# Attention and MLP on one core: a second set of row buffers, casting loads by GpSimd, and two more batches transposed by DMA

## The chip, the cores and the metric

The kernel runs on one core of a Trainium2 chip. The metric is device time in microseconds (us) from start to end of one execution. Before the change: 357.96 us, the median of three runs (357.25 to 358.84). The names of the engines are those of the profile: PE is TensorE's matrix part and PEld its weight loads, DVE is VectorE, ACT is ScalarE, POOL is GpSimd, SP is SyncE, which only issues transfers here.

## What is computed

Selective attention is followed by a layer norm and a two-layer MLP with a residual. There are 8 batches (B), 8 heads (H), 576 positions (S), 64 per head (D), so a model width of 512 and a hidden width of 2048.

```python
# attention, per batch and head
cum = np.cumsum(np.maximum(s, 0.0), axis=-1)
scores = scale * q @ k.T + np.minimum(-(cum[:, None] - cum[None, :]), 0.0)
scores = np.where(causal, -1e9, scores)
x = softmax(scores) @ v                     # heads side by side: (8, 576, 512)
# the MLP, per row
xn = (x - mean) / np.sqrt(var + 1e-6) * g_ln
out = x + np.maximum(xn @ w_ch1, 0.0) @ w_ch2
```

All inputs and the output are float32; the kernel multiplies in bfloat16.

## The kernel before, in words

**Heads and groups.** The 64 heads are numbered n = 0 to 63, eight to a batch. Four heads make a group, `gam` = 0 to 15; group `gam` serves the heads from n = 4 `gam` on. Scores need K and Q with the 64 dimensions on the partitions. They lie in `kq`, three tiles, of which two alternate (`home`, L90): group `gam` uses `kq[gam % 2]`, apart from group 2, which has `kq[2]`. Four extra rows next to the 64 carry the bias of the cumulative sum (`cT`), so one matmul of 68 rows gives score plus bias.

**Where K and Q come from.** Groups 0 to 4 (`NPE = 5`) are transposed on PE, in a start that is written out step by step (`PLAN`, L950). From group 5 on the way is: token rows (128 positions, both of k and q, four heads: a tile t; five tiles to a group, the last of 64 positions) are loaded as float32 by SyncE's queue (`ld_rows`, L170, two transfers to a tile), cast to bfloat16 into `rows[t]` by GpSimd and given their bias columns from `cT` by GpSimd (`cast_rows`, L190), and transposed by a DMA transpose of SyncE's queue into `kq` (`tr_rows`, L205, one per tile). `NHW = 16` makes this the way of all groups 5 to 15. There is one set of five row tiles: `rows` (L95) lies in `kq[2]`, which is free after group 2. Their unused columns are zeroed once (`pre(14)`, L853). A function for casting during the load by GpSimd's own queue exists (`ld_cast_rows`, L181, with `bias_of_rows`, L199), but is not reached.

**The order.** All queues run in program order, which the code writes out by hand (`manual_schedule`). The main loop (L979) goes over n from 18 to 63. For each head: `pre(n)` (loads and, by a table in n - 4 `gam`, row tiles of a coming group); the scores and their exp on ACT, and the causal mask on GpSimd (`affine_select`, L366, L396); units of the MLP; `post(n)` (casts and transposes of a coming group); one more unit; PV and its normalisation of the head two before (`pv_next`, L889); and, in the second to fourth head of a batch, the layer norm of the batch before. The remaining units that are due for this head close it (L1011).

**Tables in n - 4 `gam`.** Loads: heads -6 (tiles 0, 1), -5 (2, 3), -4 (4). Casts, in `post`: -5 (0, 1), -4 (2, 3), -3 (4). Transposes, in `post`: -4 (0, 1), -3 (2, 3, then 4). V of the next batch is cast during its load by GpSimd's queue (`ld_cast_v`, L163), one tile per head over five heads.

**The MLP as filler.** A batch gives 32 units: 16 of the first matrix (`mlp1`, L533, four matmuls of 512 columns, L537, and a relu) and 16 of the second (`mlp2`, L551, four matmuls, L555; the fourth unit of a tile adds the residual on DVE, `yo`, L564, and stores it by SyncE's queue, L582). They are spread over the heads of the next batch so that PE never runs out; `end` and `nu` (L983, L984) say how many come per head and when the next batch's units are added.

**Layer norm.** `ln_xn` (L483) makes the normalised rows `xn` of one tile on DVE (L499). For the MLP they are transposed to `xT`: on PE through PSUM with a copy (`ln_tr`, L520; matmuls at L526) for batches up to 5, by SyncE's queue (`ln_tr_dma`, L516) for batches 6 and 7. The constant `NXD = 6` decides. Where PE transposes, all five `ln_xn` come in the second head of the batch (h = 1) and the transposes in the third and fourth; where the queue does, norm and transpose come together, three tiles in the second head and two in the third. Even batches have four tiles here, odd ones five: the last 64 positions of two batches share a tile.

Lines of the main loop that the change alters, before:

```python
            if b > 2 and h == 1:
                for t in range(NT):
                    ln_xn(b - 1, t)
            for t in {2: (0, 1), 3: (2, 3, 4)}.get(h, ()):
                ln_tr(b - 1, t, "act" if b == 2 else "dve")
                if t != 1 and t != 4:
                    run_units(1)
                    nu -= 1
```

Of the kernel before, what the change touches and what calls it, by code (L numbers as in the profile page):

```python
# [15 lines left out]
P = 128  # L16
# [3 lines left out]
def kernel(  # L20
# [11 lines left out]
    nc = tc.nc  # L32
    B, H, S, D = q.shape
# [6 lines left out]
    NT = NF + 1  # L40
# [3 lines left out]
    KA = D + 4  # L44
    OB, OC, OD = 512, 1024, 1536
    EW = 1664
    G = 4
    NG = BH // G
    NPE = 5
    NM = 10  # L50
    NHW = 16
    NXD = 6
    KT = 96
    QT = 6
    QP = S // QT
# [34 lines left out]
    def home(gam):  # L90
        return 2 if gam == 2 else gam % 2


    spare = kq[2].rearrange("p u h s -> p (u h s)")
    rows = [  # L95
        spare[:, i * 2 * G * P : (i + 1) * 2 * G * P].rearrange(
            "p (u h c) -> p u h c", u=2, h=G
        )
        for i in range(NT)
    ]  # L100

    er = const.tile([P, 4, EW], BF16, name="er")
    cT = const.tile([P, NT, 2, BH, 4], BF16, name="cT")
    xm = [const.tile([P, Dm], F32, name=f"xm{i}") for i in range(4)]
# [3 lines left out]
    zeros = const.tile([P, 512], BF16, name="zeros")  # L108

    rowb = const.tile([P, NT, 2 * H, KA], BF16, name="rowb")  # L110

    def copy_on(eng, out, in_):
        if eng == "act":
            nc.scalar.copy(out=out, in_=in_)
        elif eng == "dve":
            nc.vector.tensor_copy(out=out, in_=in_)  # L116
        else:
            nc.gpsimd.tensor_copy(out=out, in_=in_)


    loaded = {}
# [37 lines left out]
    def ld_cast_pair(g):  # L159
        ld_cast("k", g)  # L160
        ld_cast("q", g)
# [8 lines left out]
    def ld_rows(gam, t):  # L170
        pn = P if t < NF else TL
        b, h0 = gam // 2, (gam % 2) * G
        tmp = stage.tile([P, 2, G, D], F32, name="rowtmp", tag="st")
        for u, src in enumerate((k, q)):
            nc.sync.dma_start(  # L175
                out=tmp[0:pn, u],
                in_=src[b, h0 : h0 + G, t * P : t * P + pn, :].rearrange("h s d -> s h d"),
            )
        loaded["rows", gam, t] = tmp

    def ld_cast_rows(gam, t):  # L181
        pn = P if t < NF else TL
        b, h0 = gam // 2, (gam % 2) * G
        for u, src in enumerate((k, q)):
            nc.gpsimd.dma_start(
                out=rows[t][0:pn, u, :, 0:D],
                in_=src[b, h0 : h0 + G, t * P : t * P + pn, :].rearrange("h s d -> s h d"),
            )

    def cast_rows(gam, t):  # L190
        pn = P if t < NF else TL
        nc.gpsimd.tensor_copy(  # L192
            out=rows[t][0:pn, :, :, 0:D], in_=loaded.pop(("rows", gam, t))[0:pn]
        )
        nc.gpsimd.tensor_copy(
            out=rows[t][0:pn, :, :, D:KA], in_=cT[0:pn, t, :, gam * G : (gam + 1) * G, :]
        )

    def bias_of_rows(gam, t):  # L199
        pn = P if t < NF else TL  # L200
        nc.vector.tensor_copy(
            out=rows[t][0:pn, :, :, D:KA], in_=cT[0:pn, t, :, gam * G : (gam + 1) * G, :]
        )

    def tr_rows(gam, t):  # L205
        pn = P if t < NF else TL
        o = t * 2 * G * P
        nc.sync.dma_start_transpose(  # L208
            out=kq[home(gam)]
            .rearrange("p u h s -> p (u h s)")[:, o : o + 2 * G * pn]  # L210
            .rearrange("p (h s) -> p h s", s=pn),
            in_=rows[t][0:pn].rearrange("p u h c -> p (u h c)"),
        )

    w1_r = moe_w_ch1.rearrange("(kd p) dh -> p kd dh", p=P)
# [6 lines left out]
    def ld_w2(i):  # L222
        nc.gpsimd.dma_start(
            out=w2_bf[:, 4 * i : 4 * i + 4, :], in_=w2_r[:, 4 * i : 4 * i + 4, :]
        )
# [3 lines left out]
    def aug(gam, eng, h0=0):  # L229
        r = slice(gam * G + h0, gam * G + G)  # L230
        i = home(gam)
        eng.dma_start(out=kq[i][D : D + 1, 1, h0:G, 0:S], in_=c_hi[r, :])
        for j in range(3):
            eng.dma_start(out=kq[i][D + 1 + j : D + 2 + j, 0, h0:G, 0:S], in_=c3[r, j, :])
# [214 lines left out]
    def x_tiles(b):  # L449
        ts_ = [xb[b][:, t, :] for t in range(NF)]  # L450
        if b % 2 == 1:
            ts_.append(xm[b // 2])
        return ts_
# [20 lines left out]
    def ln_rstd(b):  # L474
        n = len(x_tiles(b))
        rs = rstd[:, b, 0:n]
        nc.vector.tensor_scalar_add(out=rs, in0=mvs[b][:, 0:n, 1], scalar1=1e-6)  # L477
        nc.gpsimd.tensor_tensor(out=rs, in0=rs, in1=mhalf[:, 0:n], op=ALU.pow)  # L478

    def ln_aggr(b, t):  # L480
        nc.vector.bn_aggr(out=mvs[b][:, t, :], in_=st[b][:, t, 0 : 2 if b == 0 else 3, :])

    def ln_xn(b, t):  # L483
        tiles = x_tiles(b)
        if t >= len(tiles):
            return
        if b == 0:
            nc.vector.tensor_scalar(
                out=mean0[:, t : t + 1],
                in0=sum0[:, t, 0:1],  # L490
                scalar1=sum0[:, t, 1:2],
                scalar2=1.0 / Dm,
                op0=ALU.add,
                op1=ALU.mult,
            )
        else:
            ln_aggr(b, t)
        xn = xnp.tile([P, Dm], BF16, name="xn", tag="xn")
        nc.vector.scalar_tensor_tensor(  # L499
            out=xn,  # L500
            in0=tiles[t],
            scalar=mvs[b][:, t, 0:1] if b > 0 else mean0[:, t : t + 1],
            in1=gb,
            op0=ALU.subtract,
            op1=ALU.mult,
        )
        xns[b, t] = xn
        if b > 0 and t == len(tiles) - 1:
            ln_rstd(b)
# [6 lines left out]
    def ln_tr_dma(b, t):  # L516
        if (b, t) in xns:
            nc.sync.dma_start_transpose(out=xT_dst(b, t), in_=xns.pop((b, t)))
# [77 lines left out]
    def run_units(n, dve_first=False):  # L596
        for i in range(n):
            if queue:
                first_unit[0] = dve_first and i == 0
                queue.pop(0)()  # L600
# [28 lines left out]
    for i in range(2):  # L629
# [9 lines left out]
        out=maskT,  # L639
        in_=maskT,  # L640
# [209 lines left out]


    def pre(n):
        if n == 14:  # L853
            for r in rows:
                nc.gpsimd.memset(r[:, :, :, KA:P], 0.0)
        if n in PAIR_LOADS:
            ld_cast_pair(PAIR_LOADS[n])
        if n in (11, 12):
            ld_w2(n - 9)
        if n in (8, 9):  # L860
            aug(n - 5, nc.sync)
        for gam in range(NPE, NG):
            m = n - 4 * gam
            ts_ = {-6: (0, 1), -5: (2, 3), -4: (4,)}.get(m, ())
            for t in ts_:
                if gam < NHW:
                    ld_rows(gam, t)
                else:
                    ld_cast_rows(gam, t)
                    bias_of_rows(gam, t)  # L870
            if gam >= NHW:
                for t in {-4: (0, 1), -3: (2, 3, 4)}.get(m, ()):
                    tr_rows(gam, t)
        for nb in range(2, B):
            t = n - H * nb + (5 if nb == 2 else 6)
            if 0 <= t < NT:
                ld_cast_v(nb, t)

    def post(n):
        for gam in range(NPE, NHW):  # L880
            m = n - 4 * gam
# [7 lines left out]
    def pv_next():  # L889
# [5 lines left out]
        if ph_ == 7:  # L895
# [6 lines left out]
            out=c_in[:, 0:P], in0=c_in[:, 0:P], scalar=0.0, in1=eight, op0=ALU.max, op1=ALU.mult  # L902
# [24 lines left out]
            out=c_in[:, P:S], in_=c_in[:, P:S], func=ACT.Relu, scale=1.0 / scale  # L927
# [51 lines left out]
    for n in range(2 * H + 2, BH):  # L979
        b, h = n // H, n % H  # L980
        pre(n)

        end = next(m for m in [8 * i + (3 if i <= NXD else 4) for i in range(2, B)] + [BH + 3] if m >= n)  # L983
        nu = -(-len(queue) // (end - n + 1)) - 2  # L984
        scores(b, h)
        run_units(1, True)
        if h % 2 == 0:
            scores_d(b, h // 2)
        post(n)
        run_units(1)  # L990
        pv_next()
        pend.append((b, h))
        if b <= NXD:
            if n == 2 * H + 2:
                for t in range(3, NT):
                    ln_xn(1, t)
            if b > 2 and h == 1:
                for t in range(NT):
                    ln_xn(b - 1, t)
            for t in {2: (0, 1), 3: (2, 3, 4)}.get(h, ()):  # L1000
                ln_tr(b - 1, t, "act" if b == 2 else "dve")
                if t != 1 and t != 4:
                    run_units(1)
                    nu -= 1
        elif h in (1, 2):
            for t in ((0, 1, 2), (3, 4))[h - 1]:
                ln_xn(b - 1, t)
                ln_tr_dma(b - 1, t)
                run_units(1)
                nu -= 1  # L1010
        run_units(nu)  # L1011
        if n == end:
            run_units(len(queue))
            queue += batch_units(b - 1)
# [41 lines left out]
```

## Time and profile before

| | |
|---|---|
| median of three runs | 357.96 us |
| the profiled execution | 358.78 us |
| its span in the profile | 357.1 us |
| granted clock of PE | 1.00 |
| busy: PE, DVE, ACT, POOL | 349.3, 196.2, 185.5, 162.2 us |
| PE transposes of `xn` (L526) | 108 matmuls |
| casts of rows on POOL (L192) | 55 |
| row loads on SyncE (L175) | 110 issues, median 0.51 us (k), 0.53 us (q) |
| row transposes on SyncE (L208) | 55 issues, median 1.29 us |
| `xn` transposes on SyncE (L518) | 9 issues, median 1.22 us |
| a head in the main loop | about 4.6 us |

How to read it: the span is what the profiler saw of one execution; what lies around it makes the rest of that execution's own time. A busy share says how much of the span an engine had an instruction in work, not that it held anything up. What held something up is read from the waits (engine and line that waited, and what ended the wait) and from the chain that is followed back from the last instruction. SPq and POOLq are the instructions by which a queue issues transfers: the time of an issue is not the time of the transfer.

### The profile page before, as it was taken

To read this page: it belongs to the slowest core of one execution; us is meant where nothing else is said; L and a number is where in the kernel's file an instruction comes from. 1 tells how busy PE (TensorE), PEld (TensorE's weight loads), DVE (VectorE), ACT (ScalarE), POOL (GpSimd) and SP (SyncE) were. 2 spreads that over 40 slices of the span, in tenths; PEclk is the share of its full clock that TensorE was granted. 3 is DMA by queue.
4 is the path that set the end of the run, shared out by engine and by line. 5 is a ranking of instruction groups with operands and counts; after the bars stand their busy time and mean duration, and the time that the engine had idled before them with its cause. 6 is when DMAs were issued, how large, how long until landed. Compare 5 with 4: busy or idle time off the path is not lost.

```text
span 357.1 us, 8417 instructions
## 1 busy us (share of the span) xinstructions
PE 349.3 (98%) x3154; PEld 198.9 (56%) x3154; DVE 196.2 (55%) x535; ACT 185.5 (52%) x359; POOL 162.2 (45%) x344
## 2 busy tenths in 40 slices
PE   8999999999899999999999999999999999999995
PEld 3899666555455555555565555555555544444444
DVE  7788888944376536844384539543764582113111
ACT  4899886577434763267336743475366403402500
POOL 9997669458436742582556452665341010000000
PEclk9999999999999999999999999999999999999999
DMA  9999999999979998699979974999740043011013
GB/s 151 170 180 171 199 190 166 191 192 168 184 147 204 153 212 149 106 226 172 171 129 213 207 145 84 222 180 174 158 119 2 0 80 113 0 61 60 0 32 89
DMA packets 169098, 49.73 MB, mean 139 GB/s; under 512 B 157744, under 2 KB 164448, under 8 KB 169056
## 3 DMA queue, kind: packets, MB, share of 16 engines
q1 hardware_dynamic: 116016, 36.53, 53.6%
q0 software_dynamic: 51600, 11.87, 37.1%
q10 hardware_dynamic: 1440, 0.79, 0.8%
q8 instruction: 25, 0.41, 0.5%
q14 instruction: 17, 0.14, 0.1%
HBM read 37.11 MB, written 9.44 MB: 130 GB/s over the span
## 4 chain that ended last, share of the span: by engine, by line
PE 84%; DVE 6%; DMA 3%; SPq 3%; POOL 2%; issue 1%; ACT 1%; DVEq 0%; POOLq 0%; ACTq 0%
PE py L555 31%; PE ph L537 29%; PE pot L424 6%; PE sc L346 3%; PE sb L346 3%; PE sa L346 3%; PE ph L817 2%; DVE xn L499 2%; DMA kq<-kq 2%; PE st L715 2%; SPq L175 1%; DMA rowtmp<-in_q_dram 1%; PE trx L526 1%; SPq L208 1%; PE pot L773 1%
## 5 line engine op out<-in xcount | busy, mean ns | idle before, releaser
L555 PE MATMUL py<-w_bf,hT 128*128 128x512 bf16 (+1 forms) x592 | 135.5, 373 | 0.4 <-DVE yo L564 0.4
L537 PE MATMUL ph<-xT,w_bf 128*128 128x512 bf16 x480 | 114.0, 379 | 0.0
L547 ACT ACTIVATE hT<-ph 128x512 bf16<-128x512 f32 x101 | 60.2, 597 | 74.3 <-PE ph L537 74.3
L555 PEld LDWEIGHTS <-hT 128*128 128x128 bf16 x592 | 53.7, 98 | 50.7 <-issue 0.9
L537 PEld LDWEIGHTS <-w_bf 128*128 128x128 bf16 x544 | 48.7, 97 | 50.5 <-issue 3.1
L366 POOL TENSOR_SCALAR_AFFINE_SELECT er<-er 128x256 bf16<-128x256 bf16 x108 | 43.7, 419 | 53.2 <-ACT er L357 52.3
L357 ACT ACTIVATE er<-sa 128x512 bf16<-128x512 f32 x56 | 33.3, 595 | 64.9 <-PE sa L346 50.3
L545 DVE TENSOR_SCALAR hT<-ph 128x512 bf16<-128x512 f32 x35 | 24.2, 692 | 57.3 <-PE ph L537 52.4
L192 POOL CAST kq<-rowtmp 128x512 bf16<-128x512 f32 (+1 forms) x55 | 33.5, 609 | 29.3 <-DMA rowtmp<-in_q_dram 27.4
L346 PEld LDWEIGHTS <-kq 68*128 68x128 bf16 x412 | 29.7, 97 | 23.5 <-DMA kq<-kq 2.0
L424 PEld LDWEIGHTS <-er 128*128 128x128 bf16 x840 | 32.8, 98 | 11.9
L436 DVE RECIPROCAL rinv<-pot 128x5 f32<-128x5 f32 x56 | 10.7, 192 | 50.0 <-PE pot L424 49.8
L564 DVE SCALAR_TENSOR_TENSOR yo<-py,rstd,xb 128x512 f32<-128x512 f32 x32 | 24.0, 749 | 24.2 <-PE py L555 19.5
L424 PE MATMUL pot<-v_bf,er 128*128 128x65 bf16 x840 | 34.7, 194 | 0.0
L165 POOL DMA_DIRECT2D v_bf<-in_v_dram x40 | 34.4, 867 | 0.3 <-DVE kq L116 0.3
L357 ACT ACTIVATE er<-sb 128x512 bf16<-128x512 f32 x56 | 33.5, 598 | 1.3 <-PE sb L346 1.3
L357 ACT ACTIVATE er<-sc 128x512 bf16<-128x512 f32 x56 | 34.1, 610 | 0.0
L478 POOL TENSOR_TENSOR rstd<-rstd,mhalf 128x4 f32<-128x4 f32 (+1 forms) x8 | 8.9, 1115 | 45.0 <-DVE rstd L477 45.0
L438 DVE TENSOR_TENSOR xb<-pot,rinv 128x256 f32<-128x256 f32 x56 | 23.8, 424 | 1.9
L346 PE MATMUL sb<-kq 68*128 68x64 bf16 (+1 forms) x156 | 21.4, 241 | 1.7 <-DMA kq<-kq 1.7
L462 DVE BATCH_NORM_STATS2 stats<-xb 128x6 f32<-128x128 f32 (+1 forms) x84 | 21.9, 320 | 0.3
L346 PE MATMUL sc<-kq 68*128 68x256 bf16 (+1 forms) x200 | 21.7, 226 | 0.1
(116 smaller groups left out, 354.2 us busy)
## 6 DMA issues: line engine op xcount, KB each, us to landing
out_dram<-yo SPq DMA_DIRECT2D x32, 256.0 KB
rowtmp<-in_k_dram SPq DMA_DIRECT2D x44, 128.0 KB
rowtmp<-in_q_dram SPq DMA_DIRECT2D x44, 128.0 KB
v_bf<-in_v_dram POOLq DMA_DIRECT2D x32, 128.0 KB, 6.1
w_bf<-in_moe_w_ch_dram POOLq DMA_DIRECT2D x8, 512.0 KB, 9.1
kq<-kq SPq DMA_TRANSPOSE x55
kp<-in_k_dram POOLq DMA_DIRECT2D x6, 144.0 KB, 8.7
qp<-in_q_dram POOLq DMA_DIRECT2D x6, 144.0 KB, 8.8
```

Source lines behind the costliest of these rows:

```text
L165: nc.gpsimd.dma_start(out=v_bf[b % 2][:pn, t, :, 0:D], in_=v[b, :, t * P : t * P + pn, :].rearrange("h s d -> s h d"),)
L192: nc.gpsimd.tensor_copy(out=rows[t][0:pn, :, :, 0:D], in_=loaded.pop(("rows", gam, t))[0:pn])
L346: nc.tensor.matmul(a[:, c + a0 - q0 : c + a1 - q0], lhsT=k_cols(b, h, kb), rhs=cols, start=True, stop=not (pe_mask and diag),)
L357: nc.scalar.activation(out=e[:, o : o + 512], in_=a, func=ACT.Exp, scale=scale)
L366: nc.gpsimd.affine_select(out=two, in_=two, compare_op=ALU.is_ge, fill=0.0, base=0, pattern=[[0, 2], [1, P]], channel_multiplier=-1,)
L424: nc.tensor.matmul(pot[:, t, :], lhsT=e[:, o : o + P], rhs=vv[:, kb, h, :], start=(kb == 0), stop=(kb == last),)
L438: nc.vector.tensor_tensor(out=xb[b][:, :, hs], in0=pot[:, 0:NF, 0:D], in1=rinv[:, 0:NF].unsqueeze(2).to_broadcast([P, NF, D]), op=ALU.mult,)
L537: nc.tensor.matmul(ph, lhsT=w1_bf[:, kd, fb * P : (fb + 1) * P], rhs=xT[:, kd, :], start=(kd == 0), stop=(kd == KD - 1),)
L545: nc.vector.tensor_scalar_max(out=hT[:, fb, :], in0=ph, scalar1=0.0)
L547: nc.scalar.activation(out=hT[:, fb, :], in_=ph, func=ACT.Relu)
L555: nc.tensor.matmul(py[t], lhsT=hT[:, fb, t * P : (t + 1) * P], rhs=w2_bf[:, fb, c0:c1], start=(fb == 0), stop=(fb == FB - 1),)
L564: nc.vector.scalar_tensor_tensor(out=yo, in0=py[t], scalar=rs, in1=x[:, c0:c1], op0=ALU.mult, op1=ALU.add)
```

## The change

It has three parts that share constants.

- **Two sets of row tiles.** `rows` becomes two sets of five tiles: one where it was, in `kq[2]`, one in `rowb`, the row buffer of the start, which is free by then. Group `gam` uses `rows[gam % 2]`. The unused columns of both are zeroed, in `pre(13)` and `pre(15)`.
- **Casting loads from group 7 on.** `NHW` goes from 16 to 7. Groups 5 and 6 keep SyncE's loads and GpSimd's casts. Groups 7 to 15 are loaded and cast by transfers on GpSimd's queue, their bias columns are copied by DVE, and their transposes are issued in `pre` instead of `post`. Group 6's loads come one head later in program order.
- **Normalised rows of batches 4 to 7 by SyncE's queue.** `NXD` goes from 6 to 4, so batches 4 and 5 join 6 and 7. The head after which a batch's units are added (`end`) moves one head later for batches 4 and 5. For the batches that stay on PE, the norms after the first two batches are split into three tiles in the second head and two in the third, with a unit between.

```diff
-    NHW = 16
-    NXD = 6
+    NHW = 7
+    NXD = 4
...
-    rows = [
-        spare[:, i * 2 * G * P : (i + 1) * 2 * G * P].rearrange(
-            "p (u h c) -> p u h c", u=2, h=G
-        )
-        for i in range(NT)
-    ]
+    rows = [
+        flat[:, 0 : NT * 2 * G * P].rearrange("p (t u h c) -> p t u h c", t=NT, u=2, h=G)
+        for flat in (spare, rowb.rearrange("p t h c -> p (t h c)"))
+    ]
...
# in ld_cast_rows, cast_rows, bias_of_rows, tr_rows:
-                out=rows[t][0:pn, u, :, 0:D],
+                out=rows[gam % 2][0:pn, t, u, :, 0:D],
...
     def pre(n):
-        if n == 14:
-            for r in rows:
-                nc.gpsimd.memset(r[:, :, :, KA:P], 0.0)
+        if n in (13, 15):
+            for t in range(NT):
+                nc.gpsimd.memset(rows[(n // 2 + 1) % 2][:, t, :, :, KA:P], 0.0)
...
-            ts_ = {-6: (0, 1), -5: (2, 3), -4: (4,)}.get(m, ())
+            ts_ = {-6: (0, 1), -5: (2, 3), -4: (4,)}.get(m - (gam < NHW and gam > NPE), ())
...
-            if b > 2 and h == 1:
-                for t in range(NT):
-                    ln_xn(b - 1, t)
+            for t in {1: (0, 1, 2), 2: (3, 4)}.get(h, ()) if b > 2 else ():
+                ln_xn(b - 1, t)
+                if t in (1, 2, 4):
+                    run_units(1)
+                    nu -= 1
             for t in {2: (0, 1), 3: (2, 3, 4)}.get(h, ()):
                 ln_tr(b - 1, t, "act" if b == 2 else "dve")
-                if t != 1 and t != 4:
+                if t not in (1, 4) and nu > 0:
                     run_units(1)
                     nu -= 1
```

The functions that the change now reaches are in the kernel before: `ld_cast_rows` (L181) and `bias_of_rows` (L199). The table for their transposes, in `pre`, is there as well (L871 to L873): heads -4 (tiles 0, 1) and -3 (2, 3, 4).

More of the change, by code (lines that the diff above doesn't have):

```diff
@@ L192, in cast_rows @@
         nc.gpsimd.tensor_copy(
-            out=rows[t][0:pn, :, :, 0:D], in_=loaded.pop(("rows", gam, t))[0:pn]
+            out=rows[gam % 2][0:pn, t, :, :, 0:D], in_=loaded.pop(("rows", gam, t))[0:pn]
         )
         nc.gpsimd.tensor_copy(
-            out=rows[t][0:pn, :, :, D:KA], in_=cT[0:pn, t, :, gam * G : (gam + 1) * G, :]
+            out=rows[gam % 2][0:pn, t, :, :, D:KA], in_=cT[0:pn, t, :, gam * G : (gam + 1) * G, :]
         )
@@ L201, in bias_of_rows @@
         nc.vector.tensor_copy(
-            out=rows[t][0:pn, :, :, D:KA], in_=cT[0:pn, t, :, gam * G : (gam + 1) * G, :]
+            out=rows[gam % 2][0:pn, t, :, :, D:KA], in_=cT[0:pn, t, :, gam * G : (gam + 1) * G, :]
         )
@@ L211, in tr_rows @@
             .rearrange("p (h s) -> p h s", s=pn),
-            in_=rows[t][0:pn].rearrange("p u h c -> p (u h c)"),
+            in_=rows[gam % 2][0:pn, t].rearrange("p u h c -> p (u h c)"),
         )
```

## The prediction, made before the result was known

> **What bounds the kernel now.** I read the page from its first part down. TensorE (PE) is busy almost all the time, and the chain that ended last is mostly PE.
>
> ```profile
> PE 349.3 (98%) x3154; PEld 198.9 (56%) x3154; DVE 196.2 (55%) x535; ACT 185.5 (52%) x359; POOL 162.2 (45%) x344
> ...
> PE 84%; DVE 6%; DMA 3%; SPq 3%; POOL 2%; issue 1%; ACT 1%; DVEq 0%; POOLq 0%; ACTq 0%
> ```
>
> So a microsecond taken from PE's instruction list, or from a wait of PE, is a microsecond of the span; work on the other engines is free while it stays hidden. Then PE's waits, of which the largest stands alone:
>
> ```profile
> PE sb L346 <- DMA kq<-kq: 1.7, 1, 1.7
> PE idle L607 <- DVE warm L620: 1.3, 1, 1.3
> PE py L555 <- DVE yo L564: 0.4, 2, 0.2
> ```
>
> The PE timeline places the first at head n=24, the first head of group 6: the second score matmul finds the last tile's transpose not landed.
>
> ```profile
> 91.00 0.38 PE L346 MATMUL sa<-kq 68*128 68x512 bf16 x1
> 93.08 0.39 PE L346 MATMUL sb<-kq 68*128 68x64 bf16 x3 [1.71 <-DMA kq<-kq]
> ```
>
> One `sa` to the next `sb` is 0.22 us elsewhere (140.04 minus 139.82), so the stall costs 93.08 - 91.00 - 0.22 = 1.86 us. The chain, cut to 60 to 96 us, tells what made the tile late: SyncE's queue (SPq), which runs group 5's transposes, then group 6's loads, then group 6's transposes without a pause.
>
> ```profile
> 69.94 1.22 SPq L208
> 71.16 0.05 issue
> 71.21 0.57 SPq L175
> ...
> 75.24 1.88 SPq L175
> 77.16 4.14 DMA rowtmp<-in_q_dram
> ...
> 86.97 6.07 DMA kq<-kq
> 93.04 0.05 issue
> 93.08 0.39 PE sb L346 x3
> ```
>
> Next the PE timeline around head 34 (batch 3 being normalised). A tile's four PE transposes take 142.95 - 142.72 = 0.23 us of PE (0.22 at 143.81), as matmuls overlap; the 219 ns of the group's row is the length of one. The `py` after the scores starts late, because VectorE (DVE) does five `xn` in a row (140.53 to 144.9) before the `yo` that frees PE's buffer.
>
> ```profile
> 142.72 0.39 PE L526 MATMUL trx<-ident,xn 128*128 128x128 bf16 x4
> 142.95 1.03 PE L555 MATMUL py<-w_bf,hT 128*128 128x512 bf16 x4
> ...
> 145.34 0.39 PE L346 MATMUL sc<-kq 68*128 68x256 bf16 x4
> 145.94 0.81 PE L555 MATMUL py<-w_bf,hT 128*128 128x512 bf16 x3 [0.21 <-DVE yo L564]
> ```
>
> The same happens at 221.6, with batch 5. 145.94 - 145.34 against a usual 0.22 to 0.23 (140.48 - 140.25) makes 0.37 lost each time.
>
> **The change part by part.**
>
> *Normalised rows of batches 4 and 5 leave PE* (6 and 7 had left already, so "4 to 7" adds two batches). Batch 4 has 4 tiles, batch 5 has 5: 9 x 4 = 36 matmuls of L526 go; 9 x 0.225 = **-2.0 us**, all on the path, since PE is full there (55.79 of 56 us between 168 and 224). 9 copies out of PSUM on DVE (414 ns) go too, hidden. SyncE gets 9 transposes at 1.22 us (median of L518). What hides them is distance: the first unit of batch 4 now comes after head 44, that of batch 5 after head 52. Batch 6 shows the same pattern already: its transposes are issued 255.2 to 262.8, the first `ph` that reads them starts at 265.25, without a wait. If that cover went, PE would wait once per batch.
>
> The Trainium skill bears here ("VectorE: DVE Perf Modes", The three transpose paths): it gives 390 ns for a 128x128 bf16 transpose on TensorE against 1309 ns on the DMA path, and advises TensorE where PSUM will do, which speaks against this edit. By its figure, an estimate, 36 x 0.39 = 14 us would leave PE and the forecast would be about 342; the timeline's 0.23 us for four decides. The price of the slower path is paid on SyncE's queue, where this trace has its own rows.
>
> *Norms split over two heads, with a unit after them.* In the built order the `yo` now stands behind three `xn` instead of four or five. 2 x 0.37 can go; the trace gives a loss of nothing to 0.2 as the other end if another DVE order brings a new wait. I take **-0.6**.
>
> *Two row buffers, filled by GpSimd's casting transfers from group 7 on.* Removed: 90 loads on SyncE (medians 0.51 and 0.53 us) and 9 x (4 x (0.610 + 0.208) + 0.604 + 0.203) = 37 us of GpSimd (POOL) casts and copies. Added to POOL: 90 transfers. The nearest rows are a half v tile, as many 256-byte pieces (0.69 at 57.76 and at 85.11), and L157's shortest, 0.63: 9 x (8 x 0.69 + 2 x 0.65) = 61 us. POOL's net is +24 us on 89.5 of the 173 us between 95 and 268, so 66% busy. POOL's queue holds the masks, and behind a mask waits PV of that head. A head takes 4.6 us and PV runs two heads after its scores; the densest head gets 4 x 0.69 + 0.89 + 1.06 of masks = 4.7 us, the next but one 2.4. The lag stays under one head: cost 0. Also added: 45 copies on DVE, about 0.19 us each (the 187 ns of its 128x24 copy): 8.5 us minus the 9 x 0.41 above, on an engine 60% busy; they wait for transposes of two groups earlier. Cost 0.
>
> Does a group still arrive in time? Tile 4's loads issue about when its pre(4*gam-4) comes; landing takes 6.0 us (median of L165; 4.1 to 15.9), then three transposes at 1.29 and 6.07 (the landing above): 1.4 + 6.0 + 3.9 + 6.1 = 17.4 at worst in a row, against 4 heads = 18.5. The first three overlap the loads in part, so I count 3 to 5 us of margin. Cost 0; the upper end is the rival below.
>
> *Group 6.* Its loads, casts and transposes remain, but SyncE issues transposes 0 and 1 before tile 4's loads (they wait for the casts only), and group 7's ten loads leave SyncE. By the rows: queue free at 71.2; out 0.5; eight loads and an out as now, to about 78.2; two transposes to 81; tile 4's loads to 82.4; transposes 2, 3 to 85.5; the load landed at 82.4 + 4.1 = 86.5, cast and copied 87.3; transpose 4 at 87.3 with less queued ahead of it than the 6.07 had, say 4.5: 91.8, against 91.22 where PE asks. Stall 0.6 instead of 1.86. Against it: ten memsets instead of five put 5 x 0.513 = 2.6 us more on POOL before group 5's casts, in a stretch where POOL is 84% busy (16.77 of 20). If all of it comes through, the stall becomes 4.4. Ends: -1.86 and +2.6. The first transposes were slow for another reason (L208's longest, 3.64, starts at 60.8, while v loads land), so I lean to the good end: **-0.9**.
>
> *Sum:* 357.1 - 2.0 - 0.6 - 0.9 = 353.6 us of span. The profiled execution took 358.78, 1.68 outside its span, and was 0.82 above the median of 357.96. So 355.3 against the profile, **354.5** against the median.
>
> **The rivals.**
>
> *The group 6 stall is gone altogether* and nothing else shows up: 357.96 - 2.0 - 0.74 - 1.86 = 353.4. It is the good end of the forecast.
>
> *Memsets late, stall grows.* POOL's 2.6 us go through group 5's casts and SyncE's queue to head 24: 357.96 - 2.6 + 2.6 = 358.0. For it: POOL runs without a gap from 52 to 64.6. Against it: the 3.64 above, which was no cast's fault. With half of it, 356.7. Chance 0.22, no change.
>
> *It does not take PE's work away in effect*: the freed 2.0 us turn into a wait of PE for `hT` or `yo`, since ACT and DVE set the pace of the units. Then only the stalls move: 357.96 - 1.5 = 356.5. Against it: ACT is 49% busy and DVE 60% between 168 and 224. Chance 0.07, no change.
>
> *Casting transfers land late, PE waits in each group (slower).* Place: the second score matmul of heads 28, 32 to 60. In the start, where many v and weight transfers are in flight, L165 needed up to 15.9 us to land instead of 6.0. The point from which it decides is where landing exceeds 6.0 plus the 3 us of margin, about 9 us. At the price of the one stall seen, nine groups cost 9 x 1.86 = 16.7: 357.96 - 2.6 + 16.7 = 372; three groups, 361. For it: 9 x 10 more transfers on that queue. Against it: after 95 us the median is 6, and the bytes read are no more than now. Chance 0.11.
>
> **How the numbers follow.** Forecast with its good end 0.60 (its own range 352.8 to 356.3). The range runs from 352.8 to 358.2: it takes in the second and third rival and leaves out the slow one and a little below. A measurement of this kernel tells about 0.5%, 1.8 us. Faster by more 0.64, within 0.24 (some of the second rival's half-way lies in the forecast), slower 0.12.
>
> **What would show it.** L526 has 72 matmuls instead of 108; PE's busy time is 2 us lower; the wait of `py` for `yo` is gone; the wait of `sb` for `kq` at head 24 is under 1.7; no such wait at heads 28 to 60; L192 shrinks to 10, and POOL is at about 189 us (162 + 24 + 2.6). A wait of `pot` L424 for a mask would refute the POOL step, one of `ph` L537 for `xT` at heads 45 or 53 the first; a stall over 1.9 at head 24 the group 6 step.

## The result, and the profile after

The changed kernel takes **367.12 us** (median of five runs, 365.98 to 370.23) against 357.54 (five runs of the kernel before, 357.16 to 358.84): 1.026 of the time before, 95% interval 1.0227 to 1.0299. The profiled execution took 365.99, with a span of 364.3 (before 357.1). All medians, ranges and ratios, here and below, leave out runs over 1.5% above the fastest of the same kernel (three of ten of e1_end, 361.13 to 363.63 us, and one of ten of e3_pe_tr, 364.08), and a ratio can differ a little from the quotient of the medians.

First the page of the kernel after: busy times, the two queues that carry most packets, and the chain that ended last, by engine.

```profile
PE 351.5 (96%) x3118; PEld 197.8 (54%) x3118; DVE 200.6 (55%) x571; ACT 186.0 (51%) x359; POOL 197.5 (54%) x349
...
q0 software_dynamic: 94512, 17.18, 65.0%
q1 hardware_dynamic: 78000, 27.09, 41.0%
...
PE 91%; DMA 6%; DVE 1%; ACT 0%; issue 0%; SPq 0%; DVEq 0%
```

PE has 36 matmuls fewer, as planned, and is still busy 2.2 us longer. DMA now holds 6% of the chain. Of the queues (packets, MB, share of the time of 16 engines) the one that GpSimd feeds, q0, nearly doubled its share. The same two lines of before:

```profile
q1 hardware_dynamic: 116016, 36.53, 53.6%
q0 software_dynamic: 51600, 11.87, 37.1%
```

Then PE's waits after the change.

```profile
PE sb L344 <- DMA kq<-kq: 3.6, 2, 1.9
PE sa L344 <- DMA kq<-kq: 3.0, 2, 2.5
```

The stall of head 24 is gone and so are the two waits of `py` for `yo`; four new waits, 6.55 us, stand in their place. PE's timeline places the first two at head 48, the first head of group 12:

```profile
198.76 1.89 PE L535 MATMUL ph<-xT,w_bf 128*128 128x512 bf16 x8
203.12 0.57 PE L344 MATMUL sa<-kq 68*128 68x512 bf16 x1 [2.47 <-DMA kq<-kq]
205.34 0.61 PE L344 MATMUL sb<-kq 68*128 68x64 bf16 x3 [1.65 <-DMA kq<-kq]
...
206.19 1.90 PE L535 MATMUL ph<-xT,w_bf 128*128 128x512 bf16 x4
```

and the other two at head 56, the first of group 14:

```profile
242.49 1.89 PE L535 MATMUL ph<-xT,w_bf 128*128 128x512 bf16 x8
244.91 0.38 PE L344 MATMUL sa<-kq 68*128 68x512 bf16 x1 [0.53 <-DMA kq<-kq]
247.19 0.40 PE L344 MATMUL sb<-kq 68*128 68x64 bf16 x3 [1.90 <-DMA kq<-kq]
```

A second loss can be read in the first of these views: after the wait four `ph` matmuls take 1.90 us, where eight take 1.89 before it. PE runs at half its clock. The windows show it in the column PEclk, the one before DMA share and GB/s:

```profile
190.00:200.00 10.00, 10.00 (x85) 5.41 (x84) 6.91 (x20) 6.83 (x14) 9.03 (x17) 1.00 1.62 154
200.00:210.00 10.00, 5.88 (x28) 2.42 (x26) 1.79 (x7) 3.04 (x7) 4.53 (x9) 0.66 2.27 145
...
240.00:250.00 10.00, 7.56 (x55) 3.60 (x52) 2.68 (x10) 5.54 (x11) 5.29 (x10) 0.88 2.34 130
250.00:260.00 10.00, 10.00 (x81) 5.28 (x80) 4.72 (x16) 4.16 (x9) 1.10 (x3) 0.95 0.40 80
```

The trace's clock record has 0.5 from 203.2 for 6.83 us and from 247.5 for 3.41 us. Up to 205.34 PE mostly waited all the same, so of these 10.24 us about 8.1 are work at half clock, and half of that, 4.0 us, is lost.

The account closes to 0.4 us. The waits are counted from start to start, as the prediction counts its stall: `sa` is due 1.73 us after eight `ph` begin (so it goes from 196.58 to 198.31) and `sb` 0.22 us after `sa`. That makes 2.63 + 2.00 at head 48 and 0.69 + 2.06 at head 56, 7.4 us. With the clock's 4.0 the losses are 11.4; gains of 2.0 (transposes), 0.74 (`yo`) and 1.86 (head 24) make 4.6; the difference is +6.8, and the spans differ by 7.2.

**Why the tiles are late.** Two things meet at heads 48 and 56. The first lies on the side that asks: heads became short. Four heads took 18.41 us before; now head 48 asks 15.98 us after head 44 (203.12 - 2.47 - 184.67). The starts of `sa` show heads 43 and 44 as short as 2.85 and 2.04 us, because the filler had run out (only one block of `py` between them):

```profile
181.82 0.38 PE L344 MATMUL sa<-kq 68*128 68x512 bf16 x1
...
184.67 0.38 PE L344 MATMUL sa<-kq 68*128 68x512 bf16 x1
...
185.34 1.03 PE L553 MATMUL py<-w_bf,hT 128*128 128x512 bf16 x4
...
186.71 0.38 PE L344 MATMUL sa<-kq 68*128 68x512 bf16 x1
```

The trace before has the same pair once, at heads 59 and 60, behind which batch 6's units are added one head later:

```profile
259.69 0.38 PE L346 MATMUL sa<-kq 68*128 68x512 bf16 x1
...
262.55 0.38 PE L346 MATMUL sa<-kq 68*128 68x512 bf16 x1
...
264.59 0.38 PE L346 MATMUL sa<-kq 68*128 68x512 bf16 x1
```

Ahead of head 56 the heads are less short: 17.71 us from head 52 to the asking (244.91 - 0.53 - 226.67), against 18.41 before.

The second lies on the side that delivers. The transposes of group 12 land 7.6 to 10.2 us after their issue (issued 185.1 to 196.3, landed 192.7 to 205.3); before they took 3.4 to 5.9. SyncE's timeline shows the crowding too: three issues take 7.36 us, at a median of 1.29 each before.

```profile
190.16 7.36 SPq L206 DMA_TRANSPOSE kq<-kq  x3
```

On GpSimd's queue, in the same microseconds, stand the casting row loads (L183) and the v tiles of the next batch (L163), which come beside every even group and no odd one:

```profile
188.09 0.67 POOL L183 DMA_DIRECT2D kq<-in_k_dram  x1
188.71 0.67 POOL L183 DMA_DIRECT2D kq<-in_q_dram  x1
189.32 0.97 POOL L163 DMA_DIRECT2D v_bf<-in_v_dram  x1
...
191.20 0.94 POOL L163 DMA_DIRECT2D v_bf<-in_v_dram  x1
...
192.82 0.80 POOL L183 DMA_DIRECT2D rowb<-in_k_dram  x1
```

So theory **S** (short heads, from the later `end`) and theory **L** (casting row loads and v share the DMA engines with the transposes and slow them). The experiments ask whether either is enough alone.

### The profile page after: what moved, and what is told of

The parts are those of the page before. It is cut to its first block, busy times and chain, and to the rows that moved or that the text cites. A ratio compares the mean times of both kernels' runs of the same rounds, so it can differ in the third digit from the quotient of the medians.

```text
span 364.3 us, 8365 instructions
## 1 busy us (share of the span) xinstructions
PE 351.5 (96%) x3118; PEld 197.8 (54%) x3118; DVE 200.6 (55%) x571; ACT 186.0 (51%) x359; POOL 197.5 (54%) x349
## 2 busy tenths in 40 slices
DMA packets 173992, 45.58 MB, mean 125 GB/s; under 512 B 162640, under 2 KB 169344, under 8 KB 173952
## 4 chain that ended last, share of the span: by engine, by line
PE 91%; DMA 6%; DVE 1%; ACT 0%; issue 0%; SPq 0%; DVEq 0%
PE py L553 34%; PE ph L535 31%; PE pot L422 7%; DMA kq<-kq 5%; PE sc L344 3%; PE sb L344 3%; PE sa L344 3%; PE ph L815 2%; PE st L713 2%; PE trx L524 1%; PE pot L771 1%; PE trt L691 1%; DMA c_in<-in_s_dram 1%; PE trqk L294 1%; PE st L721 1%; PE sd L380 0%
## 5 line engine op out<-in xcount | busy, mean ns | idle before, releaser
L535 PE MATMUL ph<-xT,w_bf 128*128 128x512 bf16 x480 | 117.3, 387 | 0.0
L553 PEld LDWEIGHTS <-hT 128*128 128x128 bf16 x592 | 53.6, 98 | 51.1 <-issue 0.3
L163 POOL DMA_DIRECT2D v_bf<-in_v_dram x40 | 35.5, 891 | 0.0
L344 PE MATMUL sa<-kq 68*128 68x512 bf16 x56 | 21.5, 384 | 3.1 <-DMA kq<-kq 3.0
L497 DVE SCALAR_TENSOR_TENSOR xn<-xb,mv,gb 128x512 bf16<-128x512 f32 x28 | 22.6, 806 | 1.0
```

Of the source, the lines that this page charges most:

```text
L163: nc.gpsimd.dma_start(out=v_bf[b % 2][:pn, t, :, 0:D], in_=v[b, :, t * P : t * P + pn, :].rearrange("h s d -> s h d"),)
L344: nc.tensor.matmul(a[:, c + a0 - q0 : c + a1 - q0], lhsT=k_cols(b, h, kb), rhs=cols, start=True, stop=not (pe_mask and diag),)
L497: nc.vector.scalar_tensor_tensor(out=xn, in0=tiles[t], scalar=mvs[b][:, t, 0:1] if b > 0 else mean0[:, t : t + 1], in1=gb, op0=ALU.subtrac ...
L535: nc.tensor.matmul(ph, lhsT=w1_bf[:, kd, fb * P : (fb + 1) * P], rhs=xT[:, kd, :], start=(kd == 0), stop=(kd == KD - 1),)
L553: nc.tensor.matmul(py[t], lhsT=hT[:, fb, t * P : (t + 1) * P], rhs=w2_bf[:, fb, c0:c1], start=(fb == 0), stop=(fb == FB - 1),)
```

## The experiments

The runs of the kernel before that stand beside these had medians of 358.0 (first four) and 358.32 (the next four).

### e1_end: the units added as early as before

```diff
-        end = next(m for m in [8 * i + (3 if i <= NXD else 4) ...
+        end = next(m for m in [8 * i + (3 if i <= 6 else 4) ...
```

> The changed kernel, but batches 4 and 5 add their MLP units after the head they had before (43 and 51 instead of 44 and 52). Theory S (the heads before 48 and 56 became shorter, because the units of the batch before run out a head too early, so groups 12 and 14 are due before their transposes have landed): heads 44 to 47 take 18.3 us again instead of 15.6, the waits of PE at heads 48 and 56 shrink from 6.6 us together to under 1.5, the granted clock stays at 1.00, and the time is 353 to 356 us. Theory L (the casting transfers slow the DMA transposes, whatever the heads take): transposes of group 12 still need 18 to 20 us from the first issue to the last landing, PE waits over 4 us in sum, the clock falls again, 362 us or more. A third outcome: PE waits for xT at heads 44 and 52 instead.

Measured: 358.24 us (seven runs, 355.26 to 360.58), ratio 1.0005 (0.9968 to 1.0043), above the 353 to 356 that theory S expected. No wait for `kq` is listed any more in its profile (span 355.6, clock 1.0), but one for `xT`, the third outcome, is:

```profile
PE ph L535 <- DMA xT<-xn: 1.1, 1, 1.1
PE py L553 <- DMA w_bf<-in_moe_w_ch_dram: 0.4, 1, 0.4
```

With the units back one head earlier the waits of this size are gone, so S is needed for them, and about 9 us come back. But the landings are as long as after the change (up to 9.7 us in group 12), and the last tile lands within 0.2 us of PE's asking in groups 6, 10, 12 and 14. With no margin each execution can fall differently; that the spread of 5.3 us comes from there is argued, not shown.

### e2_hwloads: SyncE's loads and GpSimd's casts for all groups

```diff
-    NHW = 7
+    NHW = 16
...
-            ts_ = {...}.get(m - (gam < NHW and gam > NPE), ())
+            ts_ = {...}.get(m - (gam == 6), ())
```

> The changed kernel, but all groups are loaded by SyncE's queue and cast by GpSimd as before; two sets of row tiles and the transposes of batches 4 and 5 by DMA stay, and so do the later heads for their units. Theory L: without casting transfers a transpose lands 3.5 to 6 us after its issue at all groups, no wait of PE above 1 us at heads 48 and 56, clock 1.00, 353 to 356 us. Theory S: heads 44 to 47 still take 15.6 us, SyncE's queue (10 loads more per group) is no faster than before, PE waits 3 us or more in sum at heads 48 and 56, and the time is 358 to 364 us.

Measured: 361.14 us (359.34 to 364.3), ratio 1.0089 (1.0055 to 1.0124). The short heads are still there (2.9 and 2.0 us), but the waits for `kq` shrink to 0.7 us; two others come:

```profile
PE py L553 <- DMA w_bf<-in_moe_w_ch_dram: 2.3, 1, 2.3
PE ph L535 <- DMA xT<-xn: 2.0, 1, 2.0
```

The transposes of groups 12 and 14 land 3.8 to 5.9 us after their issue again, as theory L says. But the time lies in theory S's range, and that L is necessary for the waits is not shown by this run. SyncE, with the row loads back, issues group 12's first transpose at 195.1 instead of 185.1, and the wait for `xT`, 1.97 us in head 45, puts off the asking at head 48 (17.95 us after head 44 instead of 15.98). The last tile landed 0.4 us ahead of the asking; without that other wait it would have been 1.6 us late. And the casting transfers had a use: without them `xT` is late.

### e3_pe_tr: batches 4 and 5 on PE again

```diff
-    NXD = 4
+    NXD = 6
```

> The changed kernel, but batches 4 and 5 are transposed on PE again (108 matmuls of that line), which also puts their units back to heads 43 and 51; two sets and casting transfers stay. Theory S: no wait of PE at heads 48 and 56, clock 1.00, and against the kernel before only the stall at head 24 and the late residual sums are gone: 355 to 356 us. Theory L: even groups still need 16 us or more for their transposes (group 8 of the changed kernel took 16.3 us and was in time by 0.6), so PE waits at heads 40, 48 and 56 by 0 to 3 us each: 357 to 363 us.

Measured: 360.58 us (nine runs, 358.23 to 363.54), ratio 1.0073 (1.0034 to 1.0112). `end` is then the one of before, heads are full, and still tiles come late: 0.19 and 1.73 us at head 24 (group 6, which has no casting loads of its own), 0.58 at head 40, 0.8 at head 56. L has a price without S.

### e4_warm: PE kept busy ahead of heads 48 and 56

```diff
+        keep_warm({48: 20, 56: 13}.get(n, 0)) if n in (48, 56) else None
         scores(b, h)
```

> The changed kernel with 20 idle matmuls of 512 columns (4.3 us) ahead of head 48's scores and 13 (2.8 us) ahead of head 56's, on zeros, into a buffer nobody reads; results are the same. It fills PE's two waits without shortening them. If the clock's fall after a wait is a cost of its own (10.2 us at half speed, so 5.1 us lost): clock 1.00, 360 to 362 us against 366 to 367. If the loss is the wait alone and the clock only follows: 366 us or more.

Measured: 365.39 us (four runs, 365.13 to 367.55), ratio 1.0215 (1.0168 to 1.0261), clock 1.00. The clock no longer falls, so its fall comes from PE's idleness. How much it cost (5.1 us in the expectation, 4.0 by the account above) is not settled by this run, and neither expected time came: the fill took 4.48 and 2.97 us where the waits ahead of `sa` were 2.47 and 0.53, and its start lost another 1.2 us to the second matrix's weights.

### e5_vlate: v out of the even groups' way

```diff
 (with the edit of e1_end)
-            t = n - H * nb + (5 if nb == 2 else 6)
-            if 0 <= t < NT:
-                ld_cast_v(nb, t)
+            m = n - H * nb
+            for t in (m + 5,) if nb == 2 else {-2: (0, 1), -1: (2, 3), 0: (4,)}.get(m, ()):
+                if 0 <= t < NT:
+                    ld_cast_v(nb, t)
```

> The changed kernel with the units of batches 4 and 5 added one head earlier again (as in e1_end), and the v tiles of a batch loaded in three heads (two, two, one) from two heads before the batch instead of one per head from six heads before it. So v no longer lies beside the row transposes of an even group. Theory L (the transfers share the 16 DMA engines, and v beside the casting row loads is what makes the transposes of even groups slow): their landing falls from 7 to 9 us after the issue to 5 to 6 us, the margin of the last tile of groups 8, 10, 12, 14 grows from about 0 to 2 us or more, and the runs lie closer together than the 355.3 to 363.6 of e1_end, near 355 to 357. Rival Q (SyncE issues them late, v is innocent): landing stays at 7 to 9 us and the spread stays. Rival C (the casting row loads alone are enough): landing 6.5 to 8 us, the spread a little smaller.

Measured: **356.48 us** (seven runs, 354.76 to 357.77), ratio **0.9926 (0.9898 to 0.9954)**: 0.7% under the kernel before, and clear of the noise. No wait for `kq` at all:

```profile
PE py L553 <- DMA w_bf<-in_moe_w_ch_dram: 1.2, 1, 1.2
PE ph L535 <- DMA xT<-xn: 0.9, 1, 0.9
...
PE pot L422 <- DMA v_bf<-in_v_dram: 0.3, 1, 0.3
```

Landing and margin of the last tile, read from the trace's transfers (us; the margin is PE's asking minus the landing):

```
group           8     10    12    14     runs lie within
before         2.3    2.0   4.2   3.1    3.4 (16 runs)
after          0.8    1.7  -2.0  -2.0    4.3
e1_end         1.2    0.0  -0.1  -0.2    5.3
e5_vlate       6.8    7.0   4.8   2.9    3.0
landing, worst tile of the group
after          8.1    7.2  10.2  10.0
e1_end         8.1    8.3   9.7   8.7
e5_vlate       4.9    4.5   7.2   6.8
```

e5_vlate differs from e1_end in v alone, and its worst tiles land 1.9 to 3.8 us sooner. Odd groups, beside which v now lies, can pay: group 7's worst tile takes 9.6 us instead of 6.4, and its margin falls from 4.0 to 1.7.

The windows of the even groups 8 and 12 show what was moved. DMA share is the last column but one. Before, after, e1_end and e5_vlate, in this order:

```profile
112.00:131.00 19.00, 19.00 (x165) 10.34 (x164) 9.81 (x27) 13.03 (x26) 10.40 (x25) 1.00 1.43 190
...
188.00:207.00 19.00, 19.00 (x165) 10.35 (x164) 9.78 (x28) 12.97 (x26) 11.02 (x27) 1.00 1.35 208
```

```profile
111.00:129.00 18.00, 18.00 (x160) 9.87 (x159) 10.01 (x29) 12.73 (x25) 16.27 (x29) 1.00 1.86 146
...
185.00:203.00 18.00, 15.65 (x148) 8.57 (x145) 11.43 (x35) 11.74 (x23) 15.59 (x28) 1.00 1.63 149
```

```profile
111.00:129.60 18.60, 18.60 (x162) 10.13 (x161) 10.19 (x30) 12.83 (x25) 16.74 (x29) 1.00 1.87 147
...
186.00:205.50 19.50, 18.44 (x162) 10.00 (x160) 10.04 (x31) 12.84 (x25) 17.26 (x30) 1.00 1.98 152
```

```profile
112.00:131.00 19.00, 18.84 (x161) 10.33 (x163) 10.26 (x32) 12.80 (x25) 14.89 (x27) 1.00 1.50 149
...
187.00:207.00 20.00, 19.00 (x162) 10.33 (x163) 10.95 (x33) 12.96 (x25) 16.26 (x28) 1.00 1.64 163
```

After the change the engines carry more packet time (1.86 against 1.43 for group 8) and move less (146 against 190 GB/s). From e1_end to e5_vlate it falls from 1.87 to 1.50 and from 1.98 to 1.64. This sum is a sign of crowding and not a share of what the engines can do: packets in flight together all count, and it passes 1 in all of these windows. L holds, rival Q falls: SyncE's order is the same in e1_end and e5_vlate. Rival C holds in small: group 14's last tile still takes 6.8 us. Whether v alone would do, with the units left one head later, is not known.

### e6_start: the zeroing where it was

```diff
 (with the edit of e1_end)
-        if n in (13, 15):
+        if n in (14, 18):
             for t in range(NT):
-                nc.gpsimd.memset(rows[(n // 2 + 1) % 2][:, t, :, :, KA:P], 0.0)
+                nc.gpsimd.memset(rows[1 if n == 14 else 0][:, t, :, :, KA:P], 0.0)
```

> e1_end with the zeroing of the row buffers put back: five memsets at head 14 as before, those of the second set at head 18, after the casts of group 5. The start is then the one of the kernel before up to head 17. Theory M (the start makes the spread: v loads behind the memsets, the second matrix's weights landing late at head 17): no wait of py for w_bf, runs within 2 us of each other, median near 355.5. Theory L (the late even groups make it): the spread of 355 to 364 stays, since the margins of the groups from 8 on are as in e1_end.

Measured: 359.45 us (ten runs, 357.12 to 361.38), ratio 1.0038 (1.001 to 1.0067). The median is no better than that of e1_end and far from 355.5, so the start is not what holds e1_end back: theory M falls. The spread is 4.3 us, against 5.3. Head 24's stall is back, with 1.57 us.

### e7_hw_end and e8_pe_only: the other parts without the casting transfers

e7_hw_end joins the edits of e1_end and e2_hwloads. e8_pe_only is the kernel before with this:

```diff
-    NXD = 6
+    NXD = 4
...
-        end = ... (3 if i <= NXD else 4) ...
+        end = ... (3 if i <= 6 else 4) ...
 (and the loop with the norms split, as in the change)
```

> All groups by SyncE's loads and GpSimd's casts as before, but two sets of row buffers, group 6 one head later, norms split, batches 4 and 5 by DMA with their units added as early as before. If the casting transfers carry the loss (theory L) and the rest of the change is good, no wait of the scores for kq over 0.5 us, the spread that of the kernel before (about 3 us), and 357.9 - 2.0 (PE transposes) - 0.74 (yo) - 1.2 to 1.86 (group 6) + 1 to 2 (xT not yet landed at heads 44 and 52) = 354.5 to 356. Rival S2 (the start's memsets cost too): 1 to 3 us more, with a wait of py for w_bf.

> The kernel before with one part of the change only: normalised rows of batches 4 and 5 by SyncE's queue, norms split over two heads, units added as early as before; one set of row buffers, SyncE's loads. The prediction's two steps say -2.0 and -0.74 with an xT wait of 0 to 2: 357.9 - 2.7 + 1 = 355.2 to 357. Rival: if SyncE's nine further transposes delay the row transposes of group 10 and 12 (tile margins of 2 and 4 us before), PE waits for kq there and the time is 357 to 360.

Measured: 366.88 us, ratio 1.023 (1.0172 to 1.0288), and 367.75 us, ratio 1.0253 (1.0213 to 1.0293). Both expectations missed, in the same way. PE waits for `xT`, and the clock falls behind it (0.985 and 0.981); PE's timeline of e8_pe_only:

```profile
189.40 1.86 PE L537 MATMUL ph<-xT,w_bf 128*128 128x512 bf16 x4 [3.31 <-issue]
...
233.15 1.89 PE L537 MATMUL ph<-xT,w_bf 128*128 128x512 bf16 x4 [4.21 <-DMA xT<-xn]
```

SyncE's queue of e8_pe_only shows why: the last tile of batch 4 (184.83) is issued behind four row loads.

```profile
181.23 1.22 SPq L518 DMA_TRANSPOSE xT<-xn  x1
182.51 0.57 SPq L175 DMA_DIRECT2D rowtmp<-in_k_dram  x1
183.13 0.50 SPq L175 DMA_DIRECT2D rowtmp<-in_q_dram  x1
...
184.83 1.19 SPq L518 DMA_TRANSPOSE xT<-xn  x1
```

It lands at 189.3, and PE had asked at 186.1. In e5_vlate no row load stands there; the four issues lie between 181.2 and 186.9, and the wait is 0.9. So the parts hang together: in the orders tried, batches 4 and 5 can leave PE early only when the row loads leave SyncE, or late at the price of short heads.

### e12_cast_notr and e13_hw_notr: the loads without any transpose beside them

```diff
-    NXD = 4
+    NXD = 8
...
     def tr_rows(gam, t):
-        ...
+        return
...
-                ln_tr_dma(b - 1, t)
+                ln_tr(b - 1, t, "dve")
...
-        if b * 2 + h // G < NPE:
+        if b * 2 + h // G < NG:
```

> The changed kernel with all transfers that transpose left out: the rows of K and Q are loaded and cast, but never brought into kq, so heads of group 5 and later compute on K and Q of groups 3 and 4 (the output is not the reference's), and all normalised rows are transposed on TensorE. It shows what the casting transfers cost the DMA engines with no transpose beside them. From the two pages, the packets of GpSimd's queue took 0.65 x 364.3 - 0.371 x 357.1 = 104 us of all 16 engines more after the change, and the row loads they replace about 42. Theory L1 (a casting piece keeps an engine busy by itself): against e13_hw_notr the queue's packet time is still some 100 us more, and the row loads still need 5 us or more to land while v is in flight. Theory L2 (the time is mostly waiting beside the transposes): 60 us or less more, and landings of 3 to 4 us. Time without any wait for kq: 357 to 361 by both.

> The partner of e12_cast_notr: the same without transposing transfers (K and Q of groups 3 and 4 stand for all later groups, the output is not the reference's), but rows loaded by SyncE's queue and cast by GpSimd for all groups. The row loads' packets on SyncE's queue should take about 42 us of all 16 engines. Time 357 to 361, no wait for kq.

Measured, one execution each: 367.31 and 365.31 us, beyond the 357 to 361 expected, since PE waits for `xn` (5.1 and 5.7 us, as all transposes of a tile now hang on DVE). What was asked is in the queue lines, e12_cast_notr first:

```profile
q0 software_dynamic: 94512, 17.18, 58.6%
q1 hardware_dynamic: 15760, 11.74, 11.2%
```

```profile
q0 software_dynamic: 51600, 11.87, 36.7%
q1 hardware_dynamic: 58672, 22.36, 27.4%
```

42912 packets moved from q1 to q0. On q0 they add 0.586 x 365.6 - 0.367 x 363.6 = 81 us of all 16 engines; on q1 they had taken 0.274 x 363.6 - 0.112 x 365.6 = 59. Per packet that is 81 x 16 / 42.9 = 30 ns against 22. In the trace's packets between 110 and 262 us the medians are 32 ns for a piece cast from 256 to 128 bytes and 18 for a plain one. So 81 lies between the two theories: a casting piece does cost more by itself, and the rest of the 104 us I put down to sharing (between 110 and 262 us a casting piece takes 32.0 ns in the mean in e12_cast_notr and 38.9 in the kernel after). Sharing shows in the landings too, the pages' medians: 2.8 to 2.9 us without transposes; with them 5.8 to 6.2 for the odd groups' rows (`rowb`), though only 3.5 for the even groups' (`kq`, K).

## Why the prediction was wrong, point by point

- **What bounds the kernel.** Right: PE. But no line of the prediction weighed how crowded the DMA engines were. Their packet time was 53.6 + 37.1 = 90.7% of the span, and 1.35 to 1.43 in the windows of even groups, against 0.59 to 0.87 in those of odd ones.
- **Normalised rows of batches 4 and 5 leave PE, -2.0.** The matmuls went (72 left) and PE's time with them; no wait for `xT` came. But "What hides them is distance" had a price that was not counted: the later `end` that gives the distance lets the filler run out, and heads 43 and 44 shrink by 4.3 us (two of about 4.6 to 2.85 and 2.04). The trace before had this price in the very pattern that the prediction took from batch 6: heads 59 and 60 are as short there, and nothing was due behind them but group 15, whose last tile had landed at 256.7. Without the distance the price is the one of e7_hw_end and e8_pe_only.
- **Norms split, -0.6.** Right, and at its good end, 0.74: no wait of `py` for `yo`.
- **Two row buffers and casting transfers: POOL and DVE.** POOL is at 197.5 us, 189 were forecast: a casting issue takes 0.76 to 0.78 us, not 0.69. No wait of `pot` for a mask, as said. DVE's +4.4 us (forecast 8.5 - 3.7 = 4.8) stayed hidden.
- **"Does a group still arrive in time? ... Cost 0": the step that failed.** It put 17.4 us at worst against 18.5. Both terms were wrong: for group 12 it took 20.6 us from head 44 to the last landing (205.30 - 184.67), and PE asked after 15.98. The time to deliver was taken from rows where the transfers were plain (6.07 for the last transpose), and the last tiles of groups 12 and 14 took 9.0 and 9.3 us. The "3 to 5 us of margin" became -2.0. The argument that carried it, "the bytes read are no more than now", was true and beside the point: bytes fell (49.73 to 45.58 MB of packets) while packet time rose from 90.7% to 106% of the span.
- **Group 6, -0.9.** The stall went entirely, 1.86. That the two sets did it is not shown: e8_pe_only has one set and no stall either, and e3_pe_tr and e6_start have two sets and stalls of 1.73 and 1.57. Where the last tile lands within 2 us of the asking, a single profile tells little.
- **The slow rival** had the right mechanism and 0.11. Its place was too wide (not every group from 7 on, but the two even groups behind short heads) and its price too small: 1.86 us a group was taken from a stall that the clock survived. Group 12 cost 4.6 us of waits, from start to start, and 2.3 of clock. Its test, loads landing later than 9 us, looked at the wrong transfer: the loads' medians (5.8 to 6.2, and 3.5) stayed near the 6.0 that the prediction took, or under it; the transposes behind them went from 3.4-5.9 to 7.6-10.2.
- **Memsets late**, and **freed PE time turns into waits for `hT` or `yo`**: neither happened.

What stays open: PE's wait for the second matrix's weights at head 17 (none before and after; 1.2 us in e5_vlate, 2.3 in e2_hwloads, 1.5 and 1.0 in the last two). None of the three profiles with the zeroing in its old place shows it, seven of the nine others do; but in e2_hwloads the issue of these weights is already 0.7 us late at 37 us, ahead of anything that the change moved. And e5_vlate gains 1.8 us by the medians and 2.7 by the ratio, less than the 4.6 that the transposes, the two `yo` waits and head 24 make; its waits for weights, `xT` and v, 2.4 us, are about the difference, but no run took them away.

## What to carry to other kernels

When transfers change queue or kind, look at the 16 DMA engines as well as at the issuing engine: packets times time per packet, stage by stage, beside what already lies there. Bytes alone pointed the wrong way here. A deadline has two sides: an edit that takes filler away from the waiting engine brings the deadline forward as surely as a slow transfer misses it. Where several parts of a change lean on each other, try each alone and in pairs before one is kept; here two parts lost 8 to 10 us without the third, and moving a fourth transfer, v, with the units one head earlier again, turned the loss of 2.6% into a gain of 0.7%.

## What the runs showed of the hardware

**The clock.** All waits of PE of 1.4 us and more in these profiles (with the smaller of a pair where two belong together), with the time at half clock that began in them or soon after:

```
wait, us            kernel, head or place     at half clock, us
1.45                e4_warm, 48               none
1.48                e12_cast_notr, 17         none
1.57                e6_start, 24              none
1.71                before, 24                none
1.73                e3_pe_tr, 24              none
1.77, 1.78          e13, e12, last norms      none
1.97                e2_hwloads, 45            none
2.15                e12_cast_notr, last norms 3.41
2.15                e13_hw_notr, last norms   none
2.25                e2_hwloads, 17            3.41
0.53 + 1.90         after, 56                 3.41
2.47 + 1.65         after, 48                 6.83
3.31, 4.21          e8_pe_only, 44 and 52     6.83, 6.83
3.70, 4.16          e7_hw_end, 44 and 52      3.41, 6.83
```

Up to 1.97 us nothing follows; at 2.15 (with another 0.6 us behind it in both) the clock fell in one kernel and not in the other; from 2.25 us on it always fell, for one or two stretches of 3.41 us. A stretch costs half of what PE works in it: 1.7 us at head 56, 2.3 at head 48. The Trainium skill ("TensorE: Matmul & The Clock Gate", Part 1: The HAM clock gate) describes a free-running window of 3413 ns, and the stretches of 3.41 and 6.83 us agree with it. Its rule that an idle window of about 3.4 us throttles, and its advice against gaps over about 3 us (Why this matters for your kernels), differ from these runs: waits of 2.25 and of 0.53 + 1.90 us were enough, and the measurement decides. That the window runs free would fit the two outcomes at 2.15 us.

**Queues.** SyncE's transposes were slowed by transfers that another engine had issued: with v moved on GpSimd's queue, the worst tiles of the even groups landed 1.9 to 3.8 us sooner (e1_end and e5_vlate). The Trainium skill ("DMA: Bandwidth & Descriptors", Issuing engines are not separate DMA queues) states that transfers of the scalar, sync and gpsimd engines all run on the same 16 engines and interleave. The landing of the odd groups' casting loads, 2.9 us without and 5.8 to 6.2 us with transposes beside them, agrees.
